# Pooled attention and a mixture of depths on one core: range test ahead of the last scatters, two thirds of one batch's v sums moved from TensorE to GpSimd, and a new order of all steps

## The chip, the cores and the metric

The kernel runs on one core of a Trainium2 chip. The metric is the device time of one execution in microseconds. Shown are the median of three executions and one execution taken by the hardware profiler.

## The reference

Two blocks follow each other, for 8 batches of 576 tokens; the first has 8 heads of 64 channels, the second 512 channels.

```python
def _attn_ref(q, k, v):                       # each (8, 8, 576, 64), float32
    k_p = k.reshape(B, H, Sp, pool, D).mean(axis=3)      # pool = 8: 72 keys
    v_p = v.reshape(B, H, Sp, pool, D).mean(axis=3)
    scores = scale * np.matmul(q, k_p.transpose(0, 1, 3, 2))
    scores = scores - np.max(scores, axis=-1, keepdims=True)
    attn = np.exp(scores)
    attn = attn / (np.sum(attn, axis=-1, keepdims=True) + 1e-09)
    return np.matmul(attn, v_p)

def _moe_ref(x, w_gate, w1, w2, capacity):    # x (8, 576, 512): heads side by side; capacity 128
    scores = np.einsum('bsd,d->bs', x, w_gate)
    out = x.copy()
    for b in range(B):
        top_idx = np.argpartition(-scores[b], capacity)[:capacity]
        xe = x[b, top_idx]
        ye = np.maximum(xe @ w1, 0.0) @ w2    # w1 (512, 1024), w2 (1024, 512)
        g = 1.0 / (1.0 + np.exp(-scores[b, top_idx]))
        out[b, top_idx] = x[b, top_idx] + g[:, None] * ye
    return out
```

## The kernel before

All work is written as steps. A call of `add(engine, cost, function, reads, writes, ...)` makes one step and gives it the next number; `ORDER` is a written list of all numbers, and `Plan.place` issues the steps in that list's order. Every engine works through its own steps in that order, and so do the two queues of transfers: SP issues all loads and stores, POOL (GpSimd) the gathers and the scatters. The arguments `cost`, `prio` and `late` were for the planner that made the list; they issue nothing.

A batch goes through these steps, which are named below by the function that makes them:

- `load_k`, `load_q`, `load_v`: SP loads. k comes in two transfers, q in two, v in seven (`RUNS`); v stands in a tile of three thirds t = 0, 1, 2. k has one buffer, q and v have two. A load waits for its buffer.
- `pool_k`, `k_trans`, `q_trans`: VectorE sums and transposes k and q (L419, L423, L432, L441, L452).
- `pool_v`: the eight rows of a pool are summed, a third at a time. For the batches in `V_PE` TensorE does it, with eight matmuls by the identity a third into PSUM (L494); `copies` then brings each third to SBUF on ScalarE (L516). For the other batches POOL does it in three additions a third (L499, L503, L507). `gates` multiplies by the gate's weights (L522, on VectorE behind TensorE's sums, on POOL behind its own), VectorE adds that up (L526), and ScalarE spreads the third into the operand `VP` (L530).
- `scores(b, h, s)`: 24 small matmuls in TensorE's mode of 32 by 32 tiles (L467), then exp on ScalarE (L478, L475).
- `attend(b, c)`, c = 0 to 4: six matmuls (L557; the last chunk has 64 columns), the row sums on ScalarE (L572), the division on VectorE (L579, L583: `norm`), a store of the chunk (L590).
- `rank(b)`: VectorE adds up the scores (`score`, L599), they are laid out as a row (by TensorE's transposes, L628, in batches 0, 1 and 7, or through DRAM, L615 to L619, in the others), VectorE counts (L640), makes the one-hot matrix (L645), TensorE picks the tokens (`pick`, L652), VectorE and POOL make the indices (L656, L660), and POOL issues the gather of 128 rows of the batch's output (L661). The gather waits until the batch's five stores have landed.
- `dense(b)`: the gathered rows are turned (L686), multiplied by w1 (L695, eight groups `up`) and by w2 (L705, eight groups `down`), the result is gated and added (L710, `end`; `invert` makes the gate, L674), and POOL issues the scatter (`put`, L714).
- `range_test`: when all row sums and ranks are there, VectorE tests them (L737, L738, L742), TensorE adds over partitions (L744), and VectorE makes `flag` (L748, L749). At the end every engine reads `flag` (L40) and branches (L41) around a general path that is not taken.

The dense steps of one batch are mixed with the attention of the batches two ahead. In the list before, VectorE's last steps are

```
ranks | end of batch 6 | invert and end of batch 7 | test, verdict
```

and TensorE's last step is the matmul of L744, behind the last `down`.

Of the kernel before, what the change touches and what calls it, by code (L numbers as in the profile page):

```python
# [16 lines left out]
def kernel(  # L17
# [34 lines left out]
    53, 54, 2, 34, 32, 55, 33, 37, 56, 51, 36, 35, 1, 0, 4, 38, 5, 6, 64, 7, 8, 50, 39, 65, 9, 66, 77, 10, 11,  # L52
    67, 12, 68, 63, 13, 14, 61, 15, 89, 70, 16, 71, 17, 78, 18, 60, 19, 20, 97, 74, 21, 57, 22, 42, 62, 72, 96,
    80, 23, 24, 48, 59, 88, 25, 73, 46, 26, 47, 58, 27, 43, 28, 44, 69, 29, 40, 30, 52, 31, 90, 162, 163, 45,
    105, 164, 49, 91, 165, 41, 166, 170, 79, 92, 98, 106, 168, 180, 93, 3, 76, 107, 256, 167, 95, 94, 169, 86,
    245, 99, 253, 113, 119, 114, 85, 108, 115, 109, 118, 250, 101, 110, 117, 120, 116, 171, 121, 111, 174, 122,
    255, 112, 123, 251, 100, 124, 173, 254, 103, 87, 246, 102, 175, 243, 252, 125, 104, 244, 84, 128, 126, 176,
    81, 83, 283, 132, 129, 82, 130, 358, 177, 296, 356, 133, 134, 303, 178, 181, 140, 284, 136, 297, 141, 75,
    142, 311, 137, 247, 187, 304, 138, 186, 366, 249, 144, 139, 179, 145, 365, 146, 397, 357, 188, 312, 147,
    143, 248, 172, 367, 148, 194, 361, 182, 200, 195, 189, 196, 127, 149, 368, 197, 135, 201, 190, 131, 183,  # L60
    202, 150, 364, 203, 184, 362, 191, 198, 151, 199, 192, 359, 204, 363, 152, 193, 185, 209, 369, 360, 153,
    205, 257, 210, 290, 298, 258, 305, 285, 306, 211, 206, 313, 299, 289, 217, 314, 286, 424, 207, 307, 213,
    315, 310, 154, 316, 308, 300, 287, 155, 214, 302, 416, 215, 309, 156, 288, 291, 221, 317, 157, 218, 370,
    301, 292, 219, 158, 222, 223, 318, 293, 409, 159, 224, 225, 396, 469, 294, 319, 220, 425, 208, 320, 410,
    227, 470, 212, 261, 403, 411, 478, 426, 322, 262, 417, 371, 259, 228, 471, 418, 268, 427, 216, 323, 295,
    372, 263, 592, 373, 419, 402, 229, 226, 264, 420, 324, 398, 412, 428, 480, 326, 399, 404, 230, 265, 231,
    327, 400, 232, 481, 269, 328, 582, 473, 266, 413, 585, 482, 415, 260, 401, 330, 476, 233, 421, 477, 234,
    270, 479, 331, 267, 332, 472, 405, 160, 414, 235, 271, 236, 406, 334, 593, 423, 430, 483, 422, 273, 335,
    274, 272, 336, 429, 237, 275, 238, 240, 239, 338, 431, 509, 510, 340, 339, 276, 341, 432, 342, 484, 277,
    590, 529, 583, 407, 433, 591, 522, 517, 343, 278, 408, 161, 337, 594, 435, 486, 321, 485, 325, 523, 515,  # L70
    474, 374, 524, 511, 586, 375, 344, 475, 376, 588, 345, 512, 329, 279, 436, 346, 587, 377, 347, 333, 513,
    584, 437, 589, 348, 280, 695, 349, 439, 595, 537, 378, 440, 514, 441, 350, 530, 379, 281, 538, 443, 516,
    380, 539, 540, 386, 596, 444, 642, 351, 445, 381, 387, 353, 531, 541, 597, 532, 699, 382, 352, 434, 518,
    533, 696, 628, 534, 700, 525, 697, 383, 519, 598, 599, 447, 650, 622, 536, 354, 535, 384, 448, 651, 520,
    449, 385, 643, 542, 635, 526, 543, 527, 388, 528, 487, 706, 389, 488, 636, 451, 623, 521, 544, 644, 637,
    629, 652, 453, 489, 653, 454, 545, 455, 708, 624, 705, 638, 546, 701, 452, 390, 625, 709, 490, 456, 707,
    442, 645, 630, 548, 446, 654, 702, 391, 549, 703, 241, 491, 242, 450, 550, 438, 392, 808, 457, 704, 492,
    458, 811, 552, 815, 493, 748, 710, 809, 810, 393, 551, 553, 749, 656, 812, 626, 655, 394, 646, 755, 554,
    499, 627, 494, 736, 756, 556, 459, 500, 557, 647, 558, 495, 648, 649, 460, 631, 712, 461, 560, 462, 501,
    561, 496, 632, 562, 463, 563, 502, 464, 639, 555, 465, 564, 640, 497, 698, 641, 466, 849, 467, 547, 633,  # L80
    498, 816, 735, 750, 817, 757, 566, 751, 657, 634, 711, 819, 737, 355, 763, 658, 567, 659, 600, 758, 660,
    503, 821, 601, 818, 468, 661, 568, 820, 861, 752, 741, 504, 662, 738, 282, 742, 602, 569, 739, 822, 862,
    823, 565, 505, 740, 663, 603, 395, 759, 664, 743, 506, 814, 764, 604, 559, 507, 765, 813, 665, 766, 744,
    666, 667, 607, 570, 668, 745, 669, 571, 572, 608, 670, 754, 671, 605, 760, 573, 609, 606, 574, 673, 767,
    612, 575, 674, 610, 825, 761, 576, 611, 746, 579, 824, 753, 769, 577, 675, 768, 578, 762, 613, 677, 770,
    876, 614, 771, 877, 747, 772, 679, 615, 868, 680, 848, 681, 774, 676, 878, 672, 863, 850, 775, 879, 776,
    864, 682, 869, 616, 851, 854, 773, 870, 713, 871, 617, 714, 678, 778, 508, 618, 779, 683, 715, 780, 852,
    855, 716, 865, 684, 866, 619, 856, 782, 620, 685, 717, 783, 853, 784, 720, 686, 718, 687, 721, 719, 872,
    786, 580, 688, 875, 874, 722, 787, 857, 788, 880, 882, 689, 725, 692, 690, 693, 790, 691, 873, 723, 867,
    881, 726, 724, 791, 792, 858, 727, 793, 883, 794, 785, 728, 884, 885, 859, 795, 777, 887, 860, 781, 789,  # L90
    729, 888, 889, 826, 730, 827, 796, 891, 797, 581, 828, 798, 892, 893, 731, 829, 799, 732, 800, 895, 733,
    801, 830, 831, 833, 832, 802, 896, 838, 897, 834, 803, 804, 899, 839, 900, 835, 901, 840, 805, 902, 694,
    903, 836, 898, 904, 886, 841, 837, 890, 621, 894, 905, 921, 906, 842, 922, 806, 907, 843, 908, 909, 923,
    910, 844, 911, 924, 912, 845, 807, 925, 846, 926, 913, 928, 914, 927, 929, 915, 933, 916, 918, 917, 966,
    930, 934, 931, 935, 932, 936, 734, 937, 943, 938, 944, 939, 945, 940, 847, 946, 941, 947, 950, 948, 951,
    949, 942, 952, 955, 953, 956, 954, 957, 919, 920, 958, 959, 960, 961, 962, 963, 965, 964, 967, 968,
# [55 lines left out]
def direct_path(ctx, tc, q, k, v, moe_w_gate, moe_w1, moe_w2, moe_capacity, out, flag):  # L152
# [12 lines left out]
    NT = 3  # L165
# [21 lines left out]
    add = plan.add  # L187
# [17 lines left out]
    VS = [sb(f"vs{t}", [128, 2, E]) for t in range(NT)]  # L205
# [277 lines left out]
    def pool_v(b):  # L483
        plan.at("pool_v", b)
        for t in range(NT):
# [4 lines left out]
            if b in V_PE:  # L490
                def sums(t=t, x=x):
                    o = pA[:, 0, 2 * D * t : 2 * D * (t + 1)].rearrange("p (s d) -> p s d", s=2)
                    for w in range(POOLW):
                        nc.tensor.matmul(o, ident, x[:, :, w], start=(w == 0), stop=(w == POOLW - 1), skip_group_check=True)  # L494
                add("PE", 1.8, sums, runs_of(b, t) + ["ident"], [key, ("pAv", t)] + ["pA"] * (t == 0), 100 * b - 40)
                continue
# [37 lines left out]
    V_PE = (0, 1)  # L534
# [621 lines left out]
```

## Time and profile before

| | us |
|---|---|
| median of 3 executions | 268.93 (267.95 to 269.05) |
| the profiled execution | 268.29 |
| its span, first to last instruction | 266.4 |
| its time outside the span | 1.9 |
| TensorE busy | 244.2 |
| VectorE busy | 166.6 |
| GpSimd busy | 85.6 |
| granted TensorE clock, mean of the span | 0.988 |

Matmuls overlap: a group of matmuls is shown as busy for a little longer than the time from its start to the start of the next group. Where the text speaks of the step of a group, it is that distance between starts.

### The profile page before, as it was taken

To read this page: it belongs to the slowest core of one execution; us is meant where nothing else is said; L and a number is where in the kernel's file an instruction comes from. 1 tells how busy PE (TensorE), PEld (TensorE's weight loads), DVE (VectorE), ACT (ScalarE), POOL (GpSimd) and SP (SyncE) were. 2 spreads that over 40 slices of the span, in tenths; PEclk is the share of its full clock that TensorE was granted. 3 is DMA by queue.
4 is the path that set the end of the run, shared out by engine and by line. 5 is a ranking of instruction groups with operands and counts; after the bars stand their busy time and mean duration, and the time that the engine had idled before them with its cause. 6 is when DMAs were issued, how large, how long until landed. Compare 5 with 4: busy or idle time off the path is not lost.

```text
span 266.4 us, 7059 instructions
## 1 busy us (share of the span) xinstructions
PE 244.2 (92%) x2876; PEld 176.4 (66%) x2876; DVE 166.6 (63%) x390; ACT 89.7 (34%) x258; POOL 85.6 (32%) x160
## 2 busy tenths in 40 slices
PE   5978969899999999979999999999999999999950
PEld 2356857676886669747776678667966886867720
DVE  5977796899887977783777747556723813701020
ACT  7463622673344222442225314431343023000100
POOL 2500081539300805991324750292030013032010
PEclk9999999999999999999999999999999999999995
DMA  7997996998999699474884573052016007012100
GB/s 259 311 284 248 263 254 193 344 361 257 380 303 369 172 275 307 137 246 140 270 315 115 180 223 98 2 144 80 2 41 185 0 11 237 14 39 79 39 28 25
DMA packets 19338, 48.16 MB, mean 181 GB/s; under 512 B 2249, under 2 KB 2274, under 8 KB 19298
## 3 DMA queue, kind: packets, MB, share of 16 engines
q1 hardware_dynamic: 17986, 43.44, 52.4%
q0 software_dynamic: 1312, 4.20, 4.6%
q8 instruction: 24, 0.39, 0.6%
q14 instruction: 16, 0.13, 0.2%
HBM read 36.08 MB, written 11.55 MB: 179 GB/s over the span
## 4 chain that ended last, share of the span: by engine, by line
PE 50%; DMA 13%; issue 4%; DVE 3%; SPq 3%; POOL 2%; ACT 0%; POOLq 0%; DVEq 0%
PE pX L695 17%; PE pX L705 16%; PE pA L557 10%; PE pS L467 5%; DMA xr<-out_dram,ix 5%; DMA vr<-in_v_dram 5%; SPq L279 3%; DMA kr<-in_k_dram 2%; DMA out_dram<-xs 1%; PE pX L686 1%; DVE xs L583 1%; POOL vr L499 1%; PE pM L652 0%; DVE qt L452 0%; PE pM L628 0%
## 5 line engine op out<-in xcount | busy, mean ns | idle before, releaser
L695 PEld LDWEIGHTS pX<-xg,w 128*128 128x128 f32 x512 | 63.0, 192 | 16.6 <-issue 15.8
L695 PE MATMUL pX<-xg,w 128*128 128x128 f32 x512 | 65.8, 277 | 0.0
L705 PE MATMUL pX<-w,ht 128*128 128x512 f32 x128 | 65.4, 607 | 0.0
L557 PEld LDWEIGHTS pA<-vp,et 128*128 128x128 f32 (+1 forms) x420 | 45.4, 179 | 12.1 <-issue 8.7
L557 PE MATMUL pA<-vp,et 128*128 128x132 f32 (+1 forms) x420 | 49.3, 279 | 1.5 <-ACT vp L530 0.6
L467 PE MATMUL pS<-qt,kt 32*32 32x256 f32 (+1 forms) x1440 | 44.0, 410 | 1.3 <-ACT et L478 1.1
L452 DVE STREAM_TRANSPOSE qt<-qr 128x512 f32<-128x512 f32 (+1 forms) x40 | 39.1, 1012 | 4.6 <-DMA qr<-in_q_dram 4.6
L640 DVE SCALAR_TENSOR_TENSOR cmp<-sr,sc,lat 128x576 bf16<-128x576 f32 (+1 forms) x40 | 33.2, 831 | 8.8 <-ACT sr L633 5.1
L499 POOL TENSOR_TENSOR vr<-vr 128x512 f32<-128x512 f32 x18 | 22.8, 1274 | 47.4 <-DMA vr<-in_v_dram 45.7
L478 ACT ACTIVATE et<-pS 128x768 f32<-128x768 f32 (+1 forms) x30 | 26.8, 893 | 22.5 <-PE pS L467 22.4
L467 PEld LDWEIGHTS pS<-qt,kt 32*32 32x32 f32 x1440 | 21.2, 103 | 14.5 <-issue 1.9
L583 DVE TENSOR_TENSOR xs<-pA,rz 128x512 f32<-128x512 f32 (+1 forms) x42 | 25.3, 601 | 6.5 <-DVE rz L579 4.8
L660 POOL TENSOR_SCALAR ix<-tk 128x1 int32<-128x1 f32 x8 | 2.1, 259 | 78.6 <-DVE tk L656 48.5
L705 PEld LDWEIGHTS pX<-w,ht 128*128 128x128 f32 x128 | 20.1, 190 | 10.4 <-issue 10.3
L572 ACT ACTIVATE za<-pA,eps 128x8 f32<-128x8 f32 (+1 forms) x42 | 11.1, 264 | 46.2 <-PE pA L557 46.0
L579 DVE RECIPROCAL rz<-za 128x8 f32<-128x8 f32 (+1 forms) x40 | 7.5, 188 | 27.1 <-ACT za L572 21.7
L701 ACT ACTIVATE ht<-pX 128x512 f32<-128x512 f32 x16 | 9.6, 598 | 39.6 <-PE pX L695 39.5
L530 ACT COPY vp<-vs 32x132 f32<-32x132 f32 (+2 forms) x56 | 16.3, 299 | 14.8 <-DVE vs L526 13.7
L710 DVE SCALAR_TENSOR_TENSOR y<-pX,gv,xr 128x512 f32<-128x512 f32 x8 | 6.0, 750 | 20.6 <-PE pX L705 20.6
L494 PE MATMUL pA<-vr,ident 128*128 128x128 f32 x96 | 11.9, 278 | 4.3 <-DMA vr<-in_v_dram 4.3
L419 DVE TENSOR_TENSOR kr<-kr 128x640 f32<-128x640 f32 (+1 forms) x16 | 12.6, 787 | 3.7 <-DMA kr<-in_k_dram 3.6
L494 PEld LDWEIGHTS pA<-vr,ident 128*128 128x128 f32 x96 | 11.1, 192 | 5.5 <-issue 3.5
(100 smaller groups left out, 215.4 us busy)
## 6 DMA issues: line engine op xcount, KB each, us to landing
out_dram<-xs SPq DMA_DIRECT2D x32, 256.0 KB
kr<-in_k_dram SPq DMA_DIRECT2D x8, 640.0 KB
qr<-in_q_dram SPq DMA_DIRECT2D x8, 640.0 KB
kr<-in_k_dram SPq DMA_DIRECT2D x8, 512.0 KB
qr<-in_q_dram SPq DMA_DIRECT2D x8, 512.0 KB
vr<-in_v_dram SPq DMA_DIRECT2D x8, 512.0 KB
vr<-in_v_dram SPq DMA_DIRECT2D x16, 256.0 KB
w<-in_moe_w_dram SPq DMA_DIRECT2D x4, 1024.0 KB
```

The lines of the kernel that those rows point to most:

```text
L419: e.tensor_tensor(out=x[:, :, 0:2], in0=x[:, :, 0:2], in1=x[:, :, 2:4], op=OP.add)
L452: nc.vector.transpose(out=y.rearrange("p j s (g t) -> p t j s g", t=u), in_=x)
L467: nc.tensor.matmul(banks[t][32 * qd : 32 * qd + 32, 0:n], KT[b % 2][32 * i : 32 * i + 32, j, s, 32 * r : 32 * r + 32], QT[b % 2][h][32 * i ...
L478: add("ACT", 0.2 + 2.4e-3 * n, lambda: nc.scalar.activation(et, pS[:, :, 0:n], AF.Exp, scale=exp_scale), ["pS"], [("ET", b % 2, h, s, t) f ...
L494: nc.tensor.matmul(o, ident, x[:, :, w], start=(w == 0), stop=(w == POOLW - 1), skip_group_check=True)
L499: e.tensor_tensor(out=x[:, :, 0:4], in0=x[:, :, 0:4], in1=x[:, :, 4:8], op=OP.add)
L530: nc.scalar.copy(out=VP[b % 2][a:z, :, t, E * m : E * m + E], in_=VS[t][a:z])
L557: nc.tensor.matmul(acc[s][:, 0 : NP * E].rearrange("p (m d) -> p m d", d=E)[:, p : r + 1 : r - p], ET[i][h][s][:, t, col : col + n], VP[i] ...
L583: nc.vector.tensor_tensor(out=x[:, s], in0=a[:, :, :, 0:D], in1=rz[:, s].to_broadcast([n, s.stop - s.start, NP, D]), op=OP.mult)
L640: nc.vector.scalar_tensor_tensor(cmp[0:n], SR[0:n], SC[i][0:n, c : c + 1], LAT[0:n, LAST - OFF[c] : LAST - OFF[c] + S], op0=OP.subtract, o ...
L695: nc.tensor.matmul(pX[bank][:, cap * f : cap * f + cap], w1[g][:, d, 128 * f : 128 * f + 128], XG[i][:, d, :], start=(d == 0), stop=(d == ...
L705: nc.tensor.matmul(pX[P][0:cap, :], HT[i][f // 4][:, f % 4, :], w2[f // 4][:, f % 4, :], start=(f == 0), stop=(f == FB - 1))
```

## The change

`V_PE` becomes a table of thirds. Batch 0 stays with TensorE for all three thirds; of batch 1 only the third t = 2 stays, and t = 0 and 1 go to POOL with their gates. `copies` makes the ScalarE copies only for thirds that TensorE summed. Some planning costs of TensorE's steps are lowered, and `verdict` gets `late=7.0`; neither issues an instruction. `ORDER` is a new list throughout. The number of steps goes from 969 to 971.

```diff
-            if b in V_PE:
+            if t in V_PE.get(b, ()):
                 def sums(t=t, x=x):
...
     def copies(b):
         plan.at("copies", b)
-        for t in range(NT):
+        for t in V_PE[b]:
             def copy(t=t):
                 nc.scalar.copy(out=VS[t][:, :, 0:D], in_=pA[:, 0, 2 * D * t : 2 * D * (t + 1)].rearrange("p (s d) -> p s d", s=2))
-            add("ACT", 0.3, copy, [("pAv", x) for x in range(NT)], [("VS", t)], 100 * b - 40)
+            add("ACT", 0.3, copy, [("pAv", x) for x in V_PE[b]], [("VS", t)], 100 * b - 40)
             gates(b, t, "DVE")
...
-    V_PE = (0, 1)
+    V_PE = {0: (0, 1, 2), 1: (2,)}
     V_ENG = [("POOL",) * 3] * B
...
-        add("PE", 0.95 if split else 1.43, go, [("ET", i, h, s, x) for s in range(2) for x in range(NT)]
+        add("PE", 0.82 if split else 1.35, go, [("ET", i, h, s, x) for s in range(2) for x in range(NT)]
...
-            add("PE", 0.2, turned, [("SC", i), "ident"], ["pM"], p - 70)
+            add("PE", 0.15, turned, [("SC", i), "ident"], ["pM"], p - 70)
...
-                add("PE", 0.12 * (z - a) + 0.1, spread, [("SC", i), "ident"], ["pM"], p - 70)
+                add("PE", 0.11 * (z - a) + 0.05, spread, [("SC", i), "ident"], ["pM"], p - 70)
...
-        add("PE", 0.4, pick, ["OH", ("AUX", i)], ["pM"], p - 70)
+        add("PE", 0.3, pick, ["OH", ("AUX", i)], ["pM"], p - 70)
...
-        add("PE", 0.55, turn, [("XR", x), "ident"], [f"pX{P}"], p - 15)
+        add("PE", 0.45, turn, [("XR", x), "ident"], [f"pX{P}"], p - 15)
...
-        add("DVE", 0.4, verdict, ["pM", "want"], ["flag"], 900)
+        add("DVE", 0.4, verdict, ["pM", "want"], ["flag"], 900, late=7.0)
```

What the new list does to the order of the engines, as far as it is spoken of below:

- SP loads all of batch 0 first (before, two k halves and a q half of batch 1 stood among its v). All of v of batch 4 stands ahead of the row transfer of batch 2 (before, two of its seven transfers stood behind it).
- TensorE begins with the three v sums of batch 0, then the scores (before, scores and sums alternated). Of batch 1 it has one sum.
- POOL sums thirds 0 and 1 of batch 1 as its first additions; the gather of batch 0 stands ahead of the last third of batch 2.
- VectorE ends with: ranks, test, verdict | invert and end of batch 6 | invert and end of batch 7.
- TensorE's matmul of L744 stands among the `down` groups of batch 6, and its last step is the last `down` of batch 7.

## The prediction

> **What bounds the kernel now.** I read the page's busy rows first, then the busy time by stage, TensorE's waits, its timeline, and the end of the chain.
>
> ```profile
> PE 244.2 (92%) x2876; PEld 176.4 (66%) x2876; DVE 166.6 (63%) x390; ACT 89.7 (34%) x258; POOL 85.6 (32%) x160
> ...
> GB/s 259 311 284 248 263 254 193 344 361 257 380 303 369 172 275 307 137 246 140 270 315 115 180 223 98 2 144 80 2 41 185 0 11 237 14 39 79 39 28 25
> ```
>
> TensorE (PE) is the busiest. I cut the span where the first work on batch 0 starts (12.70), at the first dense step, the turn of batch 0 (64.8), at the end of the loads' crowd (118), and at the last `down` (256.7):
>
> ```profile
> 0.00:12.70 12.70, 9.62 (x30) 3.42 (x30) 9.41 (x25) 7.30 (x9) 5.13 (x23) 1.00 0.86 291
> 12.70:64.80 52.10, 45.05 (x817) 35.03 (x818) 41.92 (x99) 26.08 (x83) 17.15 (x26) 1.00 0.92 275
> 64.80:118.00 53.20, 51.19 (x670) 37.59 (x669) 44.40 (x90) 18.55 (x55) 24.29 (x43) 1.00 0.88 282
> 118.00:256.70 138.70, 138.15 (x1362) 100.30 (x1360) 69.01 (x172) 37.72 (x112) 38.08 (x69) 1.00 0.34 107
> 256.70:266.40 9.70, 0.19 (x2) 0.09 (x2) 1.82 (x7) 0.00 (x0) 0.97 (x1) 0.67 0.11 36
> ```
>
> The columns after the length are PE, weight loads, DVE, ACT, POOL, clock, DMA share and GB/s. PE idles 7.0 us in the second row, 2.0 in the third, 0.6 in the fourth, and does next to nothing for 9.7 us at the end. So there are three stages: a start in which loads (0.92 of the DMA engines) and DVE (42 of 52) hold PE back, a long middle that is PE alone, and a tail. What PE waits for:
>
> ```profile
> PE pA L494 <- DMA vr<-in_v_dram: 4.3, 3, 2.1
> PE pX L686 <- DMA xr<-out_dram,ix: 2.5, 2, 2.0
> ...
> 38.56 3.81 PE L494 MATMUL pA<-vr,ident 128*128 128x128 f32 x32 [2.15 <-DMA vr<-in_v_dram]
> ```
>
> v in the start, and two gathers in the middle, one late by 2 us at 117.5. The tail, as the chain has it, and the branch of PE behind it:
>
> ```profile
> 254.98 1.73 PE pX L705 x4
> 256.71 0.02 issue
> 256.73 0.75 DVE y L710
> 257.48 0.24 DVE zin L737
> 257.73 0.02 issue
> 257.75 0.55 DVE zin L738 x2
> 258.30 0.04 issue
> 258.35 0.20 PE pM L744 x2
> 258.57 0.17 DVE match L748 x2
> 258.76 0.14 DVE flag L749
> ...
> L40 PEldq TENSOR_LOAD <-flag x1: 753/753/753, 258.9 to 258.9; - x1
> L41 PEldq COMPARE_BRANCH x1: 3713/3713/3713, 259.8 to 259.8; - x1
> ```
>
> The test comes behind the last result; only then does PE read the flag (0.75) and branch, for 3.71 us where the other engines take 0.05. The final handshakes start at 263.6, right when that branch is done.
>
> **The change part by part.**
>
> *Tail.* The flag is ready early, so PE reads it when its last `down` ends (256.71 here) instead of at 258.9: 2.2 us. Beside it, from the last `down`: y 0.75, scatter issue 0.97 (ended 2.0 after it), POOL's flag read 0.79, scatter landed 3.8 after it (2.8 from issue). PE's read and branch take 4.6, so PE remains last, and the gain is the whole 2.2. If the branch waits for something that starts at its own time the gain still holds; if POOL or the scatter ends last it is 2.2 less 0 to 0.8. What moves into the middle is L744, 0.19 on PE, and one change of mode, 0.10: +0.3. The 1.3 us on DVE lie between batch 7's tokens and the end of batch 6, where DVE has idle time (69 busy of 139). Cover gone, they would delay that end by 1.3 us; behind it waits only POOL's scatter of batch 6, which has 12 us until the last result. L744 itself waits on PE's queue for DVE's test, with the rest of batch 6 behind it; the tokens of batch 7 are 4 us earlier on PE, so the test is done.
>
> *v of batch 1.* PE loses two sums of 1.8 (38.56 to 42.21 for two): -3.6 us. ACT loses two copies (0.3 each), DVE two gates (0.29 each). POOL gains twice 1.27+0.73+0.46+0.44 = 5.8 us, in a stretch where it has been idle since 12.5 (first addition of before at 33.1). By the trace it is hidden if v arrives. What speaks against it is DVE:
>
> ```profile
> 58.81 1.28 POOL L499 TENSOR_TENSOR vr<-vr 128x512 f32<-128x512 f32 x1 [2.68 <-DMA vr<-in_v_dram]
> ...
> 59.06 1.31 DVE L423 TENSOR_TENSOR ks<-kr 128x256 f32<-128x256 f32 x1
> ```
>
> That DVE addition takes 0.43 elsewhere; here it ends with POOL's. The Trainium skill, SBUF — State Buffer, "Who interferes with whom", says why: a DVE instruction with two SBUF inputs and a POOL instruction that reads SBUF exclude each other for the whole instruction. By the rule at its worst all 5.8 us go onto DVE, and the start would lose what it gains. By the order, DVE does transposes (one input) and divisions out of PSUM while these additions run, which that page exempts. I take 0, bound 0 to 5.8, nearer the low end; below nothing is excluded, since an addition on POOL frees nothing that DVE uses beyond the two gates.
>
> *Mode changes.* The timeline shows a step of 0.86 for `down` and 0.96 beside a scores group or the 64-column chunk: 0.10 a change. Counting both lists from the turn of batch 0 on, 59 become 56: -0.3 us. That part of the search moves next to nothing.
>
> *Planning costs and `late`.* They issue nothing: 0.
>
> *The start under the new list.* I walk it with the trace's durations: sum of a v third 1.9, scores 1.29 or 1.50, attend 1.35 (0.83), norm 1.0 to 1.1, exp 0.8 to 0.97, count 0.82, transposes 1.0 to 1.2. Loads: the GB/s row adds up (6.66 us a number) to 5.7 MB at 20 us, 10.8 at 40, 16.8 at 60, and data is usable 1.7 us later: the last v of batch 1 is at 10.0 MB of SP's list, which gives 36.9 and 38.6, as PE saw.
>
> - All of batch 0 is 3.5 MB, usable at 14; PE warms up to 12.3 and sums to 18. Scores to 22; `VP` and exp wait on DVE and ACT, so attend 0 at 23.3 (26.5 before).
> - The next attend into pA waits for norm 0, behind four q transposes: 28 to 29. k of batch 2 (7.7 MB, 29) stands on DVE ahead of the last k step of batch 1, so scores of batch 1 at 32 (28.0 before): a new wait, later than before. SP has 10.6 MB queued by then, so the loads run on.
> - attend of batch 0 ends at 36, PE's one sum of batch 1 (9.2 MB, 35.4) is done by 39.5, where before it went to 44.3. DVE's counts of batch 0 then follow one another, its one-hot at 48 (57.7 before).
> - The gather of batch 0 needs the stores (13.6 MB, 52.8) and now stands ahead of the last v third of batch 2: three additions, DVE's total, and behind that norm 3, norm 4 and score of batch 1. That makes 58.7 for the score, and the turn of batch 0 at 60.5 against 64.82: -4.3 us.
>
> *The middle.* Steps of PE's groups behind that turn, changes included: 188.55 before, 188.25 after, plus 0.3 for L744. w1's second half is at 17.2 MB, usable at 63.3, 0.6 after PE wants it; w2's halves (19.6 and 22.1 MB) come 2 and 3 us ahead of need. Stalls of before, 2.8 us with the two gathers. In the new list the v of batch 4 is loaded in time for POOL, so the gather of batch 2 is not caught behind it; but the turn follows the pick more closely in most batches. I leave 2 us of stalls: middle -0.3 to +0.3, say 0.
>
> Sum: -4.3 + 0 - 2.2 = -6.5 on the profiled execution's 268.29 (span 266.4 and 1.9 around it): 261.8; the median stands 0.6 above the profile, so 262.4.
>
> A second rule of the Trainium skill bears on the start: TensorE: Matmul & The Clock Gate, "What's actually happening", halves the clock after an idle window of about 3.4 us, until a busy one. The row above has a wait of 2.15 us at full clock (column 1.00). My walk has gaps of up to 2.5, so 0 by the row; by the rule a gap over 3.4 costs about 1.7 us more, once or twice, which is in the range.
>
> **The rivals.**
>
> *The start gives nothing.* If DVE is held by POOL's additions, or stores and w1 come late, PE gets to the turn at 64 as before. For it: 0.92 DMA share, and the wait of scores of batch 1. Against: PE, ACT and DVE all lose work there. Then -2.2 and up to -1 remain: 266.
>
> *Gathers come late at every turn (slower).* From pick to turn PE has this much other work, before and after: batch 1 8.3 and 5.8, 2 13.2 and 8.7, 3 6.8 and 12.0, 4 9.7 and 8.2, 5 10.1 and 9.1, 6 7.9 and 6.4, 7 6.5 and 5.6. A gather takes 0.6 for the pick and token, 0.9 for index and issue, then:
>
> ```profile
> DMA to landing us min/median/max: 3.4/3.4/7.5
> ```
>
> 4.9 us with the median, 9.0 with the longest. With 3.4 nothing stalls; with 7.5 everywhere PE loses 3.2+0.3+0.8+2.6+3.4 = 10.3, and 262.4 - 2 + 10.3 = 271. It decides from about 1.5 us a batch, where the gain is gone. Against: the long ones are those at 110 and 143, in DMA traffic; after 150 the share is low.
>
> *The start gains more*, if the stores land by 50: 258.
>
> *The list changes nothing, only the tail counts*: that is the first rival.
>
> **How the numbers follow.** Main case 0.60 (260 to 265), start gives nothing 0.24 (264.5 to 268), more 0.06, gathers late 0.10 (267 to 275). The range 258 to 268 leaves out most of the last and a little of each end. One can tell about 0.5% here, 1.3 us. Faster: 0.60 + 0.06 + 0.20 = 0.86; same 0.05; slower 0.09.
>
> **What would show it.** Right: the span ends 7.5 us after PE's last `down`; L494 x64; turn of batch 0 near 60; PE idle under 3 us after it. Wrong: DVE additions of 1.2 us in the first 45 us, L686 waiting for the gather in several batches, PE's branch not the last, or POOL's additions of batch 1 starting behind 30 us.

## The result: 255.4 us, and the profile after

The changed kernel takes 255.36 us (median of 4 runs, 253.96 to 257.48) against 268.44 (267.55 to 269.05): a ratio of 0.952 with an interval of 0.945 to 0.960. It is faster by 13.1 us; the time lies 7.0 us below the forecast of 262.4 and below the range of 258 to 268. The profiled execution took 255.49, with a span of 253.7 (before: 268.29 and 266.4). The granted clock differs from run to run; the ratios leave out the runs that it disturbed most, the medians do not.

Two marks cut both traces into three stages: the turn of batch 0 (L686), and the end of the last `down` (L705). TensorE has the same work on either side of the turn in both lists, except for the two v sums ahead of it; the matmul of L744 comes behind the last `down` in before and ahead of it in after.

| us | before | after | forecast | measured |
|---|---|---|---|---|
| turn of batch 0 | 64.8 | 57.9 | -4.3 | -6.9 |
| from there to the last `down` | 191.9 | 188.7 | 0 | -3.2 |
| from there to the end | 9.7 | 7.1 | -2.2 | -2.6 |
| span | 266.4 | 253.7 | -6.5 | -12.7 |

The busy row, the clock and the traffic, from the page:

```profile
PE 241.7 (95%) x2844; PEld 172.6 (68%) x2844; DVE 169.6 (67%) x388; ACT 88.9 (35%) x256; POOL 91.8 (36%) x168
...
PEclk9999899999999999999999999999999999999996
...
GB/s 252 329 366 301 233 305 369 326 308 262 375 330 77 254 339 290 118 231 302 326 224 106 308 205 41 83 108 90 124 44 152 42 3 146 41 41 47 41 5 48
```

By the busy row TensorE lost 2.5 us of work and the span 12.7, so ten of the 12.7 are time in which TensorE stood still. GpSimd gained 6.2 us, VectorE 3.0. The first seven numbers of the traffic row, 6.34 us each, add up to 13.7 MB by 44.4 us; before, seven of 6.66 us gave 12.1 MB by 46.6.

Busy time by stage (length, then PE, weight loads, DVE, ACT, POOL, clock, DMA share, GB/s):

```profile
10.00:55.00 45.00, 41.33 (x733) 30.59 (x732) 40.07 (x84) 24.37 (x81) 23.71 (x45) 0.96 0.96 314
55.00:110.00 55.00, 55.00 (x724) 40.18 (x729) 46.45 (x98) 20.11 (x61) 25.82 (x43) 1.00 0.82 252
110.00:246.00 136.00, 136.00 (x1374) 98.70 (x1363) 76.00 (x181) 36.91 (x109) 39.69 (x70) 1.00 0.40 124
246.00:253.70 7.70, 0.58 (x2) 0.00 (x0) 0.75 (x1) 0.00 (x0) 0.97 (x1) 0.73 0.11 39
```

From 55 us to the last matmul TensorE never stops: 55.00 of 55.00 and 136.00 of 136.00. The start holds all the idle time that is left, 3.7 us, and a clock of 0.96. TensorE's waits from 10 to 246 us say the same:

```profile
PE pA L557 <- POOL vr L503: 1.4, 1, 1.4
PE pA L557 <- ACT et L478: 1.1, 1, 1.1
PE pX L467 <- issue: 0.6, 1, 0.6
PE pM L628 <- ACT sr L633: 0.6, 1, 0.6
```

The sums' wait for v (4.3 us) and the turns' wait for gathers (2.5) are gone. The tail as the chain of waits has it (start, length, engine and line):

```profile
241.43 5.17 PE pX L705 x12
246.62 0.76 DVE y L710
247.41 0.50 POOLq L40
247.92 0.70 POOL out_dram L714
```

The instructions of L40 and then of L41 (count, shortest, median and longest in ns, first and last start; PEldq is the sequencer that hands TensorE its instructions):

```profile
L40 PEldq TENSOR_LOAD <-flag x1: 491/491/491, 242.2 to 242.2; - x1
```

```profile
L41 PEldq COMPARE_BRANCH x1: 3917/3917/3917, 242.8 to 242.8; - x1
L41 DVEq EVENT_SEMAPHORE  x1: 21/21/21, 250.2 to 250.2; - x1
```

The flag is read at 242.2, 4.4 us *before* TensorE's last matmul ends. The branch takes 3.9 us (3.7 before), and is done at 246.7, with the last `down` (246.6). What is left behind the last `down` is the result (to 247.4), the scatter (issued at 247.65, landed at 250.8), and 2.9 us from there to the end of the span. In before 2.8 us followed on the end of TensorE's branch at 263.6. That the end now hangs on the scatter is read from these times; no run moves the scatter alone.

### The profile page after: what moved, and what is told of

Same layout as the page of the kernel before. It is cut to its first block, busy times and chain, and to the rows that moved or that the text cites. A ratio compares the mean times of both kernels' runs of the same rounds, so it can differ in the third digit from the quotient of the medians.

```text
span 253.7 us, 7006 instructions
## 1 busy us (share of the span) xinstructions
PE 241.7 (95%) x2844; PEld 172.6 (68%) x2844; DVE 169.6 (67%) x388; ACT 88.9 (35%) x256; POOL 91.8 (36%) x168
## 4 chain that ended last, share of the span: by engine, by line
PE 94%; DVE 2%; ACT 1%; POOL 1%; issue 0%; POOLq 0%; ACTq 0%
PE pX L695 23%; PE pX L705 23%; PE pA L557 19%; PE pS L467 16%; PE pX L299 4%; PE pA L494 3%; PE pX L557 3%; PE pX L686 1%; PE pM L628 1%; PE pM L652 1%; DVE gs L522 1%; ACT vp L530 0%; PE pM L315 0%; ACT et L478 0%; DVE y L710 0%
## 5 line engine op out<-in xcount | busy, mean ns | idle before, releaser
L695 PEld LDWEIGHTS pX<-xg,w 128*128 128x128 f32 x512 | 62.3, 192 | 13.6 <-issue 13.4
L705 PE MATMUL pX<-w,ht 128*128 128x512 f32 x128 | 64.1, 603 | 0.0
L695 PE MATMUL pX<-xg,w 128*128 128x128 f32 x512 | 64.0, 276 | 0.0
L557 PE MATMUL pA<-vp,et 128*128 128x132 f32 (+1 forms) x420 | 50.6, 283 | 2.5 <-POOL vr L503 1.4
L467 PE MATMUL pS<-qt,kt 32*32 32x256 f32 (+1 forms) x1440 | 45.2, 420 | 0.0
L499 POOL TENSOR_TENSOR vr<-vr 128x512 f32<-128x512 f32 x20 | 25.7, 1294 | 34.3 <-DMA vr<-in_v_dram 34.3
L640 DVE SCALAR_TENSOR_TENSOR cmp<-sr,sc,lat 128x576 bf16<-128x576 f32 (+1 forms) x40 | 32.5, 812 | 8.3 <-DMA sr<-row 4.5
L583 DVE TENSOR_TENSOR xs<-pA,rz 128x512 f32<-128x512 f32 (+1 forms) x42 | 25.3, 602 | 6.5 <-DVE rz L579 4.2
L705 PEld LDWEIGHTS pX<-w,ht 128*128 128x128 f32 x128 | 20.6, 191 | 10.6 <-issue 10.1
L714 POOL DMA_INDIRECT out_dram<-y,ix x8 | 8.1, 1010 | 29.9 <-DVE y L710 20.1
L419 DVE TENSOR_TENSOR kr<-kr 128x640 f32<-128x640 f32 (+1 forms) x16 | 15.7, 993 | 1.5 <-DMA kr<-in_k_dram 1.5
L503 POOL TENSOR_TENSOR vr<-vr 128x256 f32<-128x256 f32 x20 | 15.6, 787 | 0.5
```

What stands on the lines that cost most here:

```text
L419: e.tensor_tensor(out=x[:, :, 0:2], in0=x[:, :, 0:2], in1=x[:, :, 2:4], op=OP.add)
L467: nc.tensor.matmul(banks[t][32 * qd : 32 * qd + 32, 0:n], KT[b % 2][32 * i : 32 * i + 32, j, s, 32 * r : 32 * r + 32], QT[b % 2][h][32 * i ...
L499: e.tensor_tensor(out=x[:, :, 0:4], in0=x[:, :, 0:4], in1=x[:, :, 4:8], op=OP.add)
L503: e.tensor_tensor(out=x[:, :, 0:2], in0=x[:, :, 0:2], in1=x[:, :, 2:4], op=OP.add)
L557: nc.tensor.matmul(acc[s][:, 0 : NP * E].rearrange("p (m d) -> p m d", d=E)[:, p : r + 1 : r - p], ET[i][h][s][:, t, col : col + n], VP[i] ...
L583: nc.vector.tensor_tensor(out=x[:, s], in0=a[:, :, :, 0:D], in1=rz[:, s].to_broadcast([n, s.stop - s.start, NP, D]), op=OP.mult)
```

## The experiments

Edits are given as steps in an engine's order, by the names used above; t0, t1, t2 are the thirds of v. The kernel before ran beside them at medians of 269.48 (e1 to e4), 268.97 (e5 to e8), 268.57 (e9 to e12) and 269.56 (e13, e14). For orientation, the three stages of each profiled execution (e9 to e12 are below):

| | turn of batch 0 | to the last `down` | tail | span |
|---|---|---|---|---|
| before | 64.8 | 191.9 | 9.7 | 266.4 |
| after | 57.9 | 188.7 | 7.1 | 253.7 |
| e1, after with the test last | 58.2 | 188.5 | 9.7 | 256.4 |
| e2, before with the test ahead | 63.4 | 192.0 | 7.3 | 262.7 |
| e3, after with v of batch 1 on TensorE | 64.1 | 189.0 | 7.3 | 260.4 |
| e4, before with t0, t1 of batch 1 on GpSimd | 65.4 | 191.2 | 9.4 | 266.0 |
| e5, after with the loads mixed | 69.5 | 188.7 | 7.1 | 265.3 |
| e6, before with v of batch 4 early | 65.3 | 192.1 | 9.5 | 266.9 |
| e7, scores ahead of attend 0 | 64.4 | 188.7 | 7.3 | 260.4 |
| e8, two more steps of VectorE moved | 62.9 | 188.7 | 7.2 | 258.8 |
| e13, before with one gather early | 65.0 | 190.7 | 9.4 | 265.1 |
| e14, after with that gather late | 59.6 | 193.9 | 7.1 | 260.5 |

### The tail

e1, the kernel after:

```diff
 VectorE
-ranks, test, verdict | end of batch 6 | invert, end of batch 7
+ranks | end of batch 6 | invert, end of batch 7 | test, verdict
 TensorE
-... L744 among down of batch 6 ... last down of batch 7
+... last down of batch 7, L744
```

> The new kernel with only the range test put back behind the last result (test and verdict last on VectorE, its matmul last on TensorE). Theory A (TensorE reads the flag and branches while its last matmuls still run, so the branch of 3.9 us is hidden and the tail shrinks from 9.7 to 7.1 us): slower than the new kernel by 2.6 less 0.3, about 257.7. Rival B (the tail is set by the last scatter in both, the test costs nothing): 255.4, no change.

Measured: 257.73 (256.63 to 258.14), ratio 0.960 [0.953, 0.968]; tail 9.7 instead of 7.1.

e2, the kernel before with the opposite edit:

```diff
 VectorE
-ranks | end of batch 6 | invert, end of batch 7 | test, verdict
+ranks, test, verdict | end of batch 6 | invert, end of batch 7
 TensorE
-... last down of batch 7, L744
+... L744 ahead of the fourth down of batch 6 ...
```

> The kernel before with only the range test moved ahead: test and verdict behind the ranks, its matmul behind the third down group of batch 6. Theory A: the tail falls by 2.6 us and the middle takes 0.3 more, 266.1 against 268.4. Rival B: 268.4. Rival C (the tail's gain comes only with the new order of the scatters): between the two.

Measured: 265.97 (264.52 to 266.93), ratio 0.991 [0.983, 1.000]; tail 7.3 instead of 9.7. The tails of both pairs differ by 2.4 to 2.6 us, and the middle moves by no more than 0.3. The whole of e2 doesn't measure the tail so well: its interval reaches 1.000, and 1.4 us of the 3.7 that its span is shorter lie ahead of the first turn, where nothing was changed (there its sums waited 0.4 us for v, not 4.3). By the stages the tail is one part by itself and worth 2.4 to 2.6.

### The start: sums, order, loads

e3, the order after with `V_PE = (0, 1)`:

```diff
 TensorE
-... sum t2 of batch 1 ...
+... sums t1, t0, t2 of batch 1 ...
 GpSimd
-additions and gates of t0, t1 of batch 1
 ScalarE
+two copies of batch 1
 VectorE
+two gates of batch 1
```

> The new order with all three v sums of batch 1 on TensorE, at the place where its one sum stands, copies and gates with them; GpSimd's additions of batch 1 are gone. Theory A (two sums cost TensorE 3.6 us, and the v buffer of batch 1 is freed some 15 us later, so the loads of v of batch 3 and the stores and loads queued behind them on SP come later): 255.4 + 3.6 + 1 to 4 for the late transfers, 260 to 263; by 45 us less than 13 MB moved. Rival D (TensorE waits in the start anyway, so the sums fill its gaps): under 257. Rival E (only the TensorE time counts): 259.

Measured: 260.17 (258.07 to 263.46), ratio 0.963 [0.951, 0.974]. Two runs lie at 258.1 with a clock of 0.995, two at 262.2 and 263.5 with 0.983 and 0.971. The profile is of the run of 262.2; in its timeline (start, length, group, idle time before it and what ended that) attend takes twice its 1.35:

```profile
46.19 2.67 PE L561 MATMUL pX<-vp,et 128*128 128x132 f32 x12 [1.03 <-ACT vp L534]
```

The runs with a full clock are the better measure: 258.1 against 254.0 to 255.2 for after at 0.994, so the two sums cost some 3 to 4 us, about what they take on TensorE (3.6).

e4, the order before with t0 and t1 of batch 1 on GpSimd:

```diff
 TensorE
-sums t1, t0, t2 of batch 1
+sum t2 of batch 1
 GpSimd
+additions and gates of t0, t1 of batch 1, ahead of those of batch 2
```

> The old order with two thirds of v of batch 1 on GpSimd, as its first additions, and the third on TensorE where the last of the three stood. Theory A (work off TensorE and the buffer freed early): the sum starts when its data are there, TensorE saves 3.6 us less what it then waits, 264 to 266. Rival D (the start is bound by loads and VectorE, TensorE only waits longer): 268. Rival F (GpSimd's additions hold VectorE by the shared port): over 268.4.

Measured: 268.31 (267.5 to 271.46), ratio 1.003 [0.992, 1.013]: no gain. In this order of loads v of batch 1 comes late: GpSimd's first addition starts at 37.0 us (18.4 in after). TensorE lost the two sums (3.6 us) and found a new wait of 4.2 us for VectorE's `score` (waits from 10 to 70 us):

```profile
PE pM L632 <- DVE sc L604: 4.2, 1, 4.2
PE pA L498 <- DMA vr<-in_v_dram: 1.8, 1, 1.8
```

Behind that wait its profile has TensorE at half clock from 38.9 to 45.7 us, and all four runs have a clock of 0.968 to 0.977, so the clock has a part in the miss. So the moved sums by themselves bring nothing in the old order. The new order by itself brings more: e3's 258.1 is 8 to 11 us below four of the seven runs of the kernel before beside it (266.4 to 269.5 at clocks of 0.981 to 0.988; the other three took 271.6 to 276.0), of which its own tail and middle are 5.3 (2.4 and 2.9). In the new order the sums then bring the 3 to 4 us. What differs for them is that v of batch 1 is there by 18 us instead of 37; no run moves that alone.

e5, the order after, with the first 14 loads in the sequence of before:

```diff
 SP
-all of batch 0 | k of batch 1 | v of batch 1 ...
+k, q of batch 0 | k of batch 1, v of batch 0 mixed, a q half of batch 1 ...
```

> The new kernel with the first 14 loads of SP in the order of before: k of batch 1 and half of its q stand among v of batch 0, so all of v of batch 0 is there at 5.4 MB instead of 3.5. Theory A (the start is a chain that begins with v of batch 0; nothing behind it has room to catch up): the sums end 3 to 4 us later, the turn of batch 0 comes at 60 to 62 instead of 57.9, and the kernel takes 258 to 259.5. Rival G (the start is set by VectorE, which has its k and q earlier here): 255, the turn within 1 us.

Measured: 267.03 (266.15 to 270.35), ratio 0.999 [0.994, 1.004]. All of the gain is gone, and it is 7.5 to 9 us above what was expected. TensorE now begins with sums whose v is not there; its waits from 10 to 70 us:

```profile
PE pA L498 <- DMA vr<-in_v_dram: 7.6, 1, 7.6
PE pA L561 <- ACT et L482: 4.3, 2, 3.2
```

and the sums in its timeline:

```profile
19.11 8.04 PE L498 MATMUL pA<-vr,ident 128*128 128x128 f32 x48 [7.61 <-DMA vr<-in_v_dram]
```

The three sums then took 8.04 us where after has 5.5: behind the wait the clock was at half from 14.0 to 24.3 us. So part of what e5 lost is the clock's (0.957 to 0.971 in all ten runs). TensorE's order (sums first) and SP's (batch 0 first) are one edit in two queues. Neither can be judged alone from these runs.

Why more bytes are moved in after is seen in SP's own waits, 15 to 70 us, first before, then after:

```profile
SPq L279 <- PE pA L494: 11.0, 2, 6.7
```

```profile
SPq L279 <- DVE vs L526: 7.3, 3, 4.1
SPq L279 <- DVE ks L423: 4.0, 1, 4.0
```

Before, SP stood for 11.0 us at loads whose v buffer TensorE's sums had not yet freed (from 33.8 to 40.6 it issued nothing). In after GpSimd has read its thirds of that buffer by 24.4, and that wait is gone; SP waits at other places, up to 45 us for 10.4 us against 14.2 before. What counts for the first gather are the five stores of batch 0, which stand behind these loads in SP's queue. Their last chunk was divided by 38.7 us in before and 36.8 in after (L583); SP issued its store at 47.2 and 40.8, and the last of the five landed at 53.9 and 45.9. Of the 6.3 us by which the issue is earlier, 1.9 are earlier data and 4.4 the queue. In e3, with the sums back on TensorE, SP's wait for them is back too (6.0 us), and 12.5 MB have moved by 45.6 us. That alone proves little: e7, which has no such wait but a clock as low, moved 12.8 by then.

### The clock

The start of after has a stretch at half clock. TensorE's timeline, and then the busy time in two slices of 2 us (columns as above, the clock is the third from the end):

```profile
22.98 1.80 PE L557 MATMUL pA<-vp,et 128*128 128x132 f32 x12 [1.41 <-POOL vr L503]
24.71 2.67 PE L467 MATMUL pS<-qt,kt 32*32 32x320 f32 x48
28.44 1.62 PE L557 MATMUL pA<-vp,et 128*128 128x132 f32 x12 [1.06 <-ACT et L478]
```

```profile
24.00:26.00 2.00, 2.00 (x35) 1.11 (x38) 1.85 (x4) 0.32 (x2) 0.81 (x2) 0.55 0.53 127
26.00:28.00 2.00, 1.38 (x32) 0.28 (x14) 2.00 (x5) 0.58 (x1) 0.00 (x0) 0.59 0.84 244
```

Behind 2.0 us of idle time (0.6 and 1.41, with one matmul between) the clock column falls to 0.55, the scores take 2.67 instead of 1.5, and the next attend waits 1.06 for their exp. The trace's clock records put the half clock at 24.21 to 27.62, 3.4 us. (The 1.41 is put down to GpSimd's L503, which sums v of batch 1; attend 0 reads nothing of that. ScalarE's exp of scores 00, which it does read, ended at 22.83 and is the likelier cause.) Over ten runs of after (four, and six in e12) the time follows the clock: 254.0 to 255.2 at 0.994, 257.1 to 257.5 at 0.977 and 0.978. Two attempts first tried to shorten the idle time.

e7, the kernel after with `scores` 10 of batch 0 ahead of attend 0:

```diff
 TensorE
-scores 11, attend 0, scores 10, attend 2 (batch 0)
+scores 11, scores 10, attend 0, attend 2 (batch 0)
 ScalarE
+exp of scores 00 ahead of the last six spreads of v, exp of scores 10 ahead of attend 0's row sums
```

> The new kernel with TensorE's second scores group of the second half of batch 0 ahead of the first attend, and the exp that it waits for ahead on ScalarE. Theory A (TensorE idles 20.1 to 23.0 and then runs 3 us at half clock): the group fills the gap at full clock, but the second attend still waits for the division behind four transposes on VectorE: 254 to 255.4 with less spread over the runs. Rival I (the clock's dip costs what it costs wherever TensorE idles): 255.4.

Measured: 259.80, but from 253.78 (clock 0.995) to 262.18 (0.968). The profile is of the run of 262.18; its timeline has 1.94 us of idle time inside scores 11, and behind it scores and attend at twice their length:

```profile
22.30 0.73 PE L471 MATMUL pX<-qt,kt 32*32 32x320 f32 x1 [1.94 <-issue]
22.30 2.87 PE L471 MATMUL pS<-qt,kt 32*32 32x320 f32 x48
25.10 3.01 PE L561 MATMUL pA<-vp,et 128*128 128x132 f32 x12
```

e8 adds to e7 two steps on VectorE:

```diff
 VectorE
+division of attend 0 of batch 0 ahead of the last two of four q transposes of batch 1
+last two k steps of batch 1 ahead of a total of v of batch 1 and two additions of k of batch 2
```

> As the run with the scores ahead, and on VectorE the first division ahead of two transposes, and the last two k steps of batch 1 ahead of the additions of k of batch 2. Theory A (behind the start TensorE alone counts, and each us that it starts earlier is kept as long as w1 and the gather are in time): the second attend at 25 to 26 instead of 28.4, the turn of batch 0 at 55 to 56, the kernel at 252 to 253.5. Rival J (loads bound the start: v of batch 1 and q of batch 2 are no earlier): 255, with the wait moved to the sum of batch 1 or the second scores of batch 2.

Measured: 260.57 (260.25 to 263.81), ratio 0.980 [0.966, 0.993]. A new wait of 3.1 us came in, for the division of a later chunk. Both rearrangements missed what was expected, by 4 to 6 us (e7) and 7 to 9 (e8).

e9, e10 and e11 put matmuls of zeros into the idle stretches of after, e7 and e8 (in e9 twelve ahead of attend 0 and ten ahead of attend 2 of batch 0); e12 is after itself beside them. From the edit:

```diff
         def go():
+            fill("attend", b, c)
             for t in range(NT):
...
+    def fill(*where):
+        to, n = FILL.get(where, (0, 0))
+        o = (None, pA[:, 1, 264:512], pM[:, 320:512])[to]
+        for _ in range(n):
+            nc.tensor.matmul(o, zeros[:, 0:128], zeros[:, 0 : (0, 248, 192)[to]], start=True, stop=True, skip_group_check=True)
```

> The kernel after, with idle time of TensorE in the start filled by matmuls of zeros into free columns of PSUM: 12 of 248 columns ahead of attend 0 of batch 0 (1.4 us idle there), 10 of 192 ahead of attend 2 of batch 0 (1.1 us idle). Nothing else is changed, and no other instruction waits for them. Theory (idle time of some 2 to 3 us costs TensorE a stretch of half clock; scores 10 of batch 0 took 2.67 us for that in the profile of after, and the spread of its runs is this): the rows of 24 to 28 us show a clock of 1.00, scores 10 take 1.5 us, the turn of batch 0 comes at 57 us or earlier, the median is 253.5 to 254.8 and the runs lie within 1 us of each other with a mean clock of 0.99 or more. Rival (the dips come from something else, power or the other traffic): median 255.4 and a spread of 2 to 3 us as in after's runs, with the half clock still in the rows.

> The order of e7 (scores 10 of batch 0 ahead of attend 0) with zero matmuls in its three idle stretches: 16 ahead of scores 10 of batch 0, 16 ahead of attend 2 of batch 0, 18 ahead of scores 00 of batch 1. e7's runs lay between 253.8 (clock 0.995) and 262.2 (0.968). Clock theory: every run now near the fastest of e7, median 252.5 to 254.5, clock 0.99 or more, turn of batch 0 at 56 to 58 us against 64.4. Rival (the order itself is worse, the clock only follows): median 258 to 260, the waits for VectorE at attend 2 and scores 00 of batch 1 as long as in e7 and the turn after 62.

> The order of e8 with zero matmuls in its idle stretches: 16 ahead of scores 10, 16 ahead of attend 2, 5 ahead of scores 00 of batch 1, 32 ahead of attend 4 of batch 0 (where TensorE waited 3.1 us for VectorE's division). Clock theory: no half clock in the rows to 52 us; what is left is the real wait of attend 4, worth at most 3 us, so 253.5 to 256.5 against 260.6. Rival (e8 lost by its waits alone): 259 to 261.

> The kernel after unchanged, on the same chip as the three kernels with filled idle time, for a comparison of the spread of its runs: 254 to 257.5 as before, the time falling as the mean granted clock rises (0.977 to 0.994). If all its runs are at 254 here, the fill has nothing to win.

| | median and range | turn of batch 0, profile | its clock |
|---|---|---|---|
| e12, after | 255.71 (254.08 to 257.33) | 58.1 | 0.988 |
| e9, after with fill | 257.13 (253.72 to 259.74) | 56.2 | 0.994 |
| e10, e7 with fill | 260.73 (258.6 to 262.89) | 63.0 | 0.977 |
| e11, e8 with fill | 260.14 (258.23 to 262.58) | 60.4 | 0.996 |

In e9's profile the dip is gone (the same two slices), and the execution took 253.72, the fastest of its six:

```profile
24.00:26.00 2.00, 2.00 (x55) 1.07 (x54) 1.53 (x4) 0.55 (x3) 1.11 (x3) 1.00 0.77 184
26.00:28.00 2.00, 1.87 (x19) 1.64 (x17) 1.73 (x4) 1.02 (x3) 0.00 (x0) 1.00 1.06 334
```

That is what the clock theory said of the trace: the turn comes 1.9 us earlier than in e12. But it isn't shown that the fill did it. After itself has runs of 253.96 and 254.08 at a clock of 0.994, so e9's trace may be that of a run which would have had no dip anyway; over its six runs e9's clock goes from 0.979 to 0.994, e12's from 0.977 to 0.994. The spread did not shrink, and the median is not better than after's. One run of e9 took 257.24 at a clock of 0.994, so something else moves the time by 3 us as well, and no trace of such a run is there. e10 still has a gap of 2.06 us, in the middle of scores 11, where no fill stood, and half clock behind it. e11 has no dip and is still 2.7 us of span behind after, so the order of e8 is worse for more than its dips. So the time follows the clock in after's runs, and a trace shows what one dip costs; it is not the only cause of the spread, and filling is not a version to take. None of these beats the kernel after.

### The middle

No kernel with the old list had less than 191.2 us from the first turn to the last `down`, none of the new list up to here more than 189.0 (before 191.9, after 188.7). Before, GpSimd issues the gather of batch 2 at 109.88, though its tokens were ready at 104.88 (`token`, L656): the v additions of batches 4 and 5 stand ahead of it in the queue. GpSimd's timeline of before:

```profile
104.34 1.75 POOL L503 TENSOR_TENSOR vr<-vr 128x256 f32<-128x256 f32 x2
...
107.09 1.27 POOL L499 TENSOR_TENSOR vr<-vr 128x512 f32<-128x512 f32 x1
...
109.88 1.06 POOL L661 DMA_INDIRECT xr<-out_dram,ix  x1 [0.28 <-POOL ix L660]
```

e6 tried the cause of that in SP's queue:

```diff
 SP, kernel before
-row transfer of batch 2 ... two loads of v of batch 4
+two loads of v of batch 4, row transfer of batch 2 ...
```

> The kernel before with two loads of v of batch 4 moved ahead of the row transfer of batch 2 on SP. Theory A (the gather of batch 2 was caught on GpSimd behind additions that waited for these loads): the stall of 2 us at the turn of batch 2 is gone, 266.3 against 268.4; the middle, turn of batch 0 to the last down, falls from 191.9 to 189.8. Rival H (that gather is late for another reason, such as the transfers around it): the stall stays, 268.4.

Measured: 267.36 (265.74 to 270.97), ratio 1.004 [0.999, 1.009]. The stall at the turn became waits elsewhere and the middle stayed at 192.1, so neither the theory nor its rival came out: this stall went, and the time didn't. e13 and e14 move the gather itself.

e13, the kernel before:

```diff
 GpSimd
-additions of v of batch 4, an addition of batch 5, two steps of batch 4, gather of batch 2
+two additions of v of batch 4, gather of batch 2, the rest
```

> The kernel before with one step moved: on GpSimd the gather of batch 2 stands ahead of L503 of the third of batch 4 that ran at 105.36, instead of behind seven more steps on v. Before: tokens of batch 2 ready at 104.88, gather issued 109.37 to 110.94, turn of batch 2 stalled by 1.95 us until 117.49. Theory (the middle lost 2 us because the gather stood in GpSimd's queue behind v additions): gather issued at 105 to 106.5, landed by 113, no stall at the turn of batch 2, first turn to last down 189.7 to 190.2 instead of 191.9, time 266.4 to 267. Rival A (the gather is late in the transfer queues behind the loads, wherever it is issued): it lands at 117 still, no change. Rival B (the three additions that it delays by 1.6 us hold up attend 0 of batch 4): the stall moves there, no change.

Measured: 265.47 (264.71 to 267.57), ratio 0.989 [0.983, 0.995]. The gather is issued at 107.26, and the turn of batch 2 comes at 116.5 without a wait. TensorE's waits from 66 to 250 us:

```profile
PE pS L471 <- ACT et L482: 1.1, 1, 1.1
PE pX L690 <- DMA xr<-out_dram,ix: 0.4, 1, 0.4
```

The 1.95 us went, and 1.1 came back as a wait for exp: the middle is 190.7, 1.2 better. The ratio says some 3 us; the rest isn't attributed.

e14, the kernel after, the other way:

```diff
 GpSimd
-addition of batch 5, gather of batch 2, seven steps on v of batch 5
+addition of batch 5, seven steps on v of batch 5, gather of batch 2
```

> The kernel after with one step moved: the gather of batch 2 on GpSimd behind seven steps on v of batch 5 instead of ahead of them (it was issued at 103.67 to 105.53, now at 108.3 to 110). Theory: it lands 4.4 us later, at 113.5 to 116, and the turn of batch 2 (111.7 without a wait) stalls by 2 to 4 us: first turn to last down 190.7 to 192.7, time 257.5 to 259.5. Rival (the new list leaves room for a late gather, its gain is elsewhere): no stall over 0.5 us and 255.4.

Measured: 257.94 (255.83 to 263.05), ratio 0.957 [0.950, 0.964], against 255.4 to 255.7 and 0.952 to 0.956 for after: as a time no more than hinted, since the intervals overlap. In the profiled execution (262.33) the middle is 193.9. Its waits from 66 to 250 us, and a slice behind the stall:

```profile
PE pX L690 <- DMA xr<-out_dram,ix: 3.1, 1, 3.1
```

```profile
118.00:120.00 2.00, 2.00 (x11) 2.00 (x10) 0.00 (x0) 0.20 (x1) 1.74 (x3) 0.50 1.00 379
```

The stall is back with 3.1 us, and behind it TensorE runs at half clock for 3.4 us. So one place in GpSimd's queue took away 1.2 us of the middle in the old list and brought a stall of 3.1 in the new. Issue is only part of it: the gather issued at 109.88 in before took 7.5 us to land, that of e13 3.5; in e14 it took 6.1, in after 3.4. Why the later ones land more slowly was not tested.

## Why the prediction was wrong

The direction was right, all three parts have the predicted sign or better, and the size was missed: -6.5 was worked out and -12.7 measured.

- **The tail, -2.2, measured -2.6.** The gain is about right, its reason half. "PE remains last" failed: with the flag ready early, TensorE's sequencer reads it 4.4 us before its last matmuls end, and the 3.9 us branch runs beside them. The end then hangs on the scatter. The prediction priced this case as 0 to 0.8 us *less*; it came out as a little more, because TensorE's 4.6 us no longer lie behind the last `down` at all, and the scatter is the shorter of the two. It landed 4.2 us behind the last `down`; in before TensorE's branch was done 6.9 us behind it. That 2.2 forecast and 2.6 measured lie so close is in part luck.
- **The start, -4.3, measured -6.9.** The walk held up to where the stores count: attend 0 at 23.3 (measured 22.98), one-hot at 48 (done at 46.9). The step that failed is the landing of data. It was read from the traffic row of *before*, which put 13.6 MB and with it the stores at 52.8 us. But that row contains SP's waits for TensorE's sums, which the change removes. In after 13.7 MB have moved by 44.4, and batch 0's stores had landed by 45.9. The gather of batch 0 therefore waited for its token, not for the stores, and was issued at 49.27 (GpSimd's timeline):

```profile
48.26 0.24 POOL L660 TENSOR_SCALAR ix<-tk 128x1 int32<-128x1 f32 x1 [7.30 <-DVE tk L656]
49.27 1.12 POOL L661 DMA_INDIRECT xr<-out_dram,ix  x1 [0.77 <-DMA w<-in_moe_w_dram]
```

  (The load of w named in the second line shares a counter with one of the stores; the gather starts before that load is complete, at 49.8.) Everything behind it moved along: the score of batch 1 at 54.98 (58.7 was forecast), the turn at 57.88 (60.5). The prediction gave "the stores land by 50" a chance of 0.06 as a rival; that is what happened, and its 258 was still too high, by the middle.
- **The middle, 0, measured -3.2.** The steps of TensorE's groups were right: 188.25 and 0.3 for L744 make 188.55, and 188.7 was measured. What failed is "I leave 2 us of stalls" and the 0.6 us for w1: after has none of either. The prediction had itself seen that the gather of batch 2 is not caught behind v, which removed the stall of 1.95 (e13, e14), and then kept two microseconds because "the turn follows the pick more closely", with no wait named for them. No turn waited in after. Of the 3.2, 2.55 are idle time of before; 0.3 of mode changes less and 0.3 of L744 more cancel; some 0.6 us of slightly longer steps in before are not attributed.
- **The port, 0 with a bound of 5.8.** The rule that the prediction took from the Trainium skill (SBUF — State Buffer, "Who interferes with whom") shows in after's trace, GpSimd first and then VectorE:

```profile
18.38 1.47 POOL L499 TENSOR_TENSOR vr<-vr 128x512 f32<-128x512 f32 x1 [2.94 <-DMA vr<-in_v_dram]
```

```profile
18.64 1.36 DVE L522 TENSOR_TENSOR gs<-vs,wg 128x128 f32<-128x128 f32 x1
```

  A gate of 0.28 takes 1.36 while the addition runs. This is the only such meeting ahead of attend 0, about 1 us, so 0 was a little low and the low end was right. Over the whole kernel VectorE is busy 3.0 us longer than before, but that isn't the price of the moved thirds: in e3, where GpSimd sums nothing of batch 1 and VectorE has two gates more (0.6), VectorE's 172.1 us are more than after's 169.6. In the new order k's first additions alone (L419) take 15.7 us against 12.6.
- **The clock, 0 by the row, 1.7 by the rule.** Neither fits. The Trainium skill (TensorE: Matmul & The Clock Gate, "What's actually happening") halves the clock after an idle window of about 3.4 us, and says that the window runs free, so that the same kernel differs from run to run. The prediction's row, 2.15 us at full clock, was one sample of that, and its reading of the rule wanted a gap over 3.4 us. In after 2.0 us of idle time in two pieces were enough for 3.4 us of half clock, and the scores took 1.2 us longer. The length fits the page's window: the clock records of these runs have half clock for 3.4 us, or two or three times that. That the idle time must fill a window isn't what these traces show.
- **The mode changes, -0.3**, are within what the middle can tell: 0.10 a change was the step in after too.
- **The rivals.** Gathers late at every turn did not come: GpSimd's row for the gathers of after says

```profile
DMA to landing us min/median/max: 3.4/3.5/6.5
```

  and no turn waited. e14 shows that the mechanism was real, with a price of the size that the prediction gave it for one batch (0.3 to 3.4 us; 3.1 measured), and that one place in GpSimd's queue can bring it about.
- **The signs.** Of those for right, L494 runs 64 times and TensorE stood still for none of the time behind the turn; the span ends 7.1 us behind the last `down` and the turn comes at 57.9. Of those for wrong two came: a VectorE instruction held to 1.36 us in the first 45 us, and TensorE's branch not the last.

## What to carry to other kernels

When a change removes a wait that a *load queue* stood in, don't read the landing of later data from the old traffic curve: walk the load queue again with its buffers freed at the new times. Stalls kept in a sum should each have a place and a cause; an unnamed remainder belongs into the range, not into the sum. And where one engine serves both bulk work and the short step that releases the busiest engine (here GpSimd with v additions and gathers), the order in its queue is worth checking first: one place of one step took 1.2 us from the middle in one list and brought a stall of 3.1 in the other.

## What the runs showed of the hardware that was not expected

- TensorE's sequencer reads a flag and branches while its own matmuls are still queued: read at 242.2, branch of 3.92 us from 242.8, last `down` ended at 246.6. Nothing is seen of this branch behind the last `down` when the flag is ready long before (SP's queue read it at 228.0), and the tail is 2.6 us longer when the flag is the last thing made (e1). The other engines' branches took 0.05 to 0.07 us; why TensorE's takes 3.6 to 3.9 stays open.
- Between the start-up and the last `down`, TensorE's half clock came in stretches of 3.4 us (after, e1, e12, e13), 6.8 (e4, e7, e10, e14) or 10.2 (e5), by the clock records of the traces. Single idle stretches of about 2 us in a row of busy ones were enough to bring it: 1.85 us in e13, 1.94 in e7, 2.02 in e12. It did not come behind 1.92 in e2, nor behind 1.95 and 2.15 in the profile of before. So the length of the stretch alone doesn't decide; what does is not shown. The loss can be larger than the wait itself: e14's middle grew by 5.2 us for a wait of 3.1.
